# Another emission order for a fused linear-attention and SwiGLU kernel: every engine's queue and the load queue reordered, and casts, copies, masks and 1/rms dealt anew

## The chip, the cores and the metric

The kernel runs on one core of one Trainium2 chip. The core has five engines with a queue of their own each: TensorE (PE in the profile; its weight loads are PEld), VectorE (DVE), ScalarE (ACT), GpSimd (POOL) and SyncE (SP), which here only issues DMAs. The metric is the device time of one execution in microseconds, as the median of a few runs; lower is better.

## The reference

Inputs are r, k, v, w of shape (4, 8, 768, 48) (batch, heads, sequence, head size), u of (8, 48), and the weights of a feed-forward block, all in float32. The first half is a linear attention with a decaying state:

```python
for t in range(S):
    cur = einsum('bhd,bhe->bhde', u[None] * kt, vt)
    y[:, :, t] = einsum('bhd,bhde->bhe', rt, state + cur)
    state = wt[..., None] * state + einsum('bhd,bhe->bhde', kt, vt)
```

The heads are then laid side by side, which gives 3072 tokens of 384 features, and the second half is a gated block on them:

```python
rms = sqrt(mean(x * x, -1) + 1e-06); xn = x / rms * rms_g
g = xn @ w_gate; val = xn @ w_val            # 384 -> 1536
out = (g / (1 + exp(-g)) * val) @ w_out      # 1536 -> 384, float32
```

## The kernel before

**Tiling.** The sequence is cut into chunks of 128 positions, so there are six superblocks n = 0..5 of four batches j = 0..3, and a step n.j stands for one chunk of one batch with all eight heads. Four chunks (512 tokens) make one pass of the gated block, also numbered 0 to 5; in the first two passes the chunks are dealt otherwise: pass 0 takes 0.0, 0.1, 1.0 and 1.1, pass 1 takes 0.2, 1.2, 0.3 and 1.3. Pass 1 is done in halves of 256 tokens.

**Steps of a chunk.** `load_r`, `load_k`, `load_v`, `load_w` fetch 192 KB each on SP's queue (the w of superblocks 0 and 1 come together, 384 KB). `ln` takes log w on ScalarE, `cs_mm` sums it along the chunk on TensorE into two PSUM banks (from superblock 2 on into one, and VectorE's `cs_add` makes the other), `exp_r` and `exp_k` take exponentials, `r_mul` and `k_mul` scale r and k with them. The result is transposed to rkT: in superblocks 0 and 1 by TensorE (`rk_pe`) and a copy out of PSUM (`rk_tr`), later by a DMA transpose on SP's queue (`rk_tr` too). `q_mm` multiplies k by r, `q_mask_e` masks the even heads on VectorE, and the odd ones are either masked by VectorE (`q_mask_o`) or copied by ScalarE (`q_copy_o`) and then cut by GpSimd's select (`q_mask_o`). `cast_v` makes v bf16. `y_mm` adds the state's part and the chunk's own, `st_mm` and `st_new` carry the state on, `bonus_mul`, `bonus_sum` and `bonus_v` make the u term on GpSimd and VectorE, `x_add` joins them. Then come the square sum `x_sq` and `xn_mul` on ScalarE with 1/rms (`x_rstd`) between, and a transpose with the gain: `xn_pe` and `xn_out` up to superblock 3, a DMA transpose `xn_tr` on SP and `xn_gain` on GpSimd in 4 and 5.

**Steps of a pass.** For twelve groups f of 128 hidden units: `gate_mm` and `val_mm` (three matmuls of 512 columns each), `silu` on ScalarE, `h_mul` on VectorE. Then `o_mm` per chunk (twelve matmuls of 384 columns), `o_out` out of PSUM, `out_dma` on SP's queue. The last chunk's `o_mm` is in two halves, 5.3 and 5.4. The weights come by DMAs on GpSimd's queue: `load_gv.g.h` with g = 0 for groups 0 to 3, g = 1 for groups 4 to 11, h = 0 for gate and 1 for value, and `load_wo`.

**What sets the order.** ORDER is a list of 1056 steps written out; the kernel calls them in turn, so each engine, and SP's and GpSimd's DMA queues, gets its instructions in the order of its own steps in that list, and waits in that order. A suffix `:m` puts m filler matmuls on zeros ahead of the step's first PSUM use. PSUM banks come from three rings: two for gate and cs_r (`a`), two for value and cs_k (`b`), four for everything else (`q`); which bank a step gets is derived from the list. r, k and v have eight input buffers each.

**What deals the steps.** Sets of n.j name the engine: `CAST_ACT` puts `cast_v` on ScalarE (otherwise GpSimd), `K_POOL` puts `k_mul` on GpSimd (otherwise VectorE), `RK_DVE` the copy `rk_tr` on VectorE (otherwise ScalarE), `ODD_DVE` the odd mask on VectorE, `RSTD_ACT` 1/rms on ScalarE as exp(-0.5 ln) (otherwise GpSimd), `OUT_DVE` `o_out` on VectorE (otherwise ScalarE). SiLU lives in another activation table than logarithm and exponential; the helper `act` loads a table when the needed one changes.

Lines: loads 259 and 271, weight loads 351 and 354, casts 387 and 389, activations 251 with table loads 249, cs_mm 404 to 422, k_mul 459, rk_pe 482, rk_tr 487 to 491, q_mm 500 and 502, masks 507 to 518, st_mm 528, y_mm 545 and 548, 1/rms 566 and 567, xn_tr 580, groups 617 and 622 (halves), h_mul 643 and 646, o_mm 660, o_out 667 and 669, out_dma 677.

## Time and profile before

| | us |
|---|---|
| median of three runs | 204.41 (203.04 to 204.47) |
| profiled execution, first to last instruction (span) | 202.2 |
| what lies around the span, by the three runs | 0.8 to 2.3 |
| TensorE matmuls busy | 191.3 (95%) |
| VectorE busy | 157.5 (78%) |
| ScalarE busy | 135.0 (67%) |
| GpSimd busy | 124.4 (62%) |

The profiled execution's own time is its span; the runs' times also hold what lies around it, and the page does not say which of the runs it resembles most. A row of a timeline is the start, the length, the engine, the line, the operation, what it writes and reads, and in brackets the idle time ahead of it with what ended it. A row of a stretch has the length, then for each of the five engine columns PE, PEld, DVE, ACT and POOL the busy time and the number of instructions, then the granted TensorE clock, the share of the DMA engines and GB/s. In a row of groups the figures behind the first bar are busy microseconds and mean nanoseconds, behind the second the idle time ahead of the group and what ended it. A busy PE includes modelled ends of its pipelined matmuls, so its idle time is a lower bound.

### The profile page before, as it was taken

To read this page: it belongs to the slowest core of one execution; us is meant where nothing else is said; L and a number is where in the kernel's file an instruction comes from. 1 tells how busy PE (TensorE), PEld (TensorE's weight loads), DVE (VectorE), ACT (ScalarE), POOL (GpSimd) and SP (SyncE) were. 2 spreads that over 40 slices of the span, in tenths; PEclk is the share of its full clock that TensorE was granted. 3 is DMA by queue.
4 is the path that set the end of the run, shared out by engine and by line. 5 is a ranking of instruction groups with operands and counts; after the bars stand their busy time and mean duration, and the time that the engine had idled before them with its cause. 6 is when DMAs were issued, how large, how long until landed. Compare 5 with 4: busy or idle time off the path is not lost.

```text
span 202.2 us, 4604 instructions
## 1 busy us (share of the span) xinstructions
PE 191.3 (95%) x1677; PEld 121.9 (60%) x1694; DVE 157.5 (78%) x307; ACT 135.0 (67%) x278; POOL 124.4 (62%) x178
## 2 busy tenths in 40 slices
...
DMA  6999999999999998989899999995464013030132
GB/s 144 231 234 207 212 208 202 195 179 208 206 184 225 160 212 191 210 185 188 199 176 215 237 188 203 183 190 108 134 179 104 0 23 99 0 117 0 63 115 99
DMA packets 121567, 32.42 MB, mean 160 GB/s; under 512 B 116420, under 2 KB 120392, under 8 KB 121544
## 3 DMA queue, kind: packets, MB, share of 16 engines
...
q8 instruction: 13, 0.21, 0.4%
...
q10 hardware_dynamic: 8, 0.00, 0.0%
...
## 4 chain that ended last, share of the span: by engine, by line
PE 65%; ACT 3%; DMA 2%; DVE 2%; issue 1%; SPq 0%; DVEq 0%; ACTq 0%
PE ps_av L617 7%; PE ps_bu L617 7%; PE ps_au L617 7%; PE ps_bv L617 6%; PE ps_qx L660 6%; PE ps_qv L660 6%; PE ps_qu L660 5%; PE ps_qz L660 4%; PE ps_au L622 2%; PE ps_bu L622 2%; DMA rkT<-rk 2%; PE ps_av L622 2%; PE ps_bv L622 2%; ACT L249 1%; PE ps_au L419 1%; PE ps_qv L500 1%
## 5 line engine op out<-in xcount | busy, mean ns | idle before, releaser
L660 PEld LDWEIGHTS <-ht 128*128 128x128 bf16 x300 | 28.1, 98 | 17.5 <-DVE ht L646 1.0
L251 ACT ACTIVATE sg<-ps_av 128x512 bf16<-128x512 f32 x36 | 21.5, 597 | 22.8 <-PE ps_av L617 18.0
L646 DVE TENSOR_TENSOR ht<-ps_bv,sg 128x512 bf16<-128x512 f32 x29 | 19.9, 687 | 13.9 <-PE ps_bv L617 12.9
L251 ACT ACTIVATE sg<-ps_au 128x512 bf16<-128x512 f32 x36 | 21.5, 596 | 11.5 <-PE ps_au L617 7.7
L617 PEld LDWEIGHTS <-wg_sb 128*128 128x128 bf16 x180 | 19.2, 114 | 15.9 <-issue 0.6
L617 PEld LDWEIGHTS <-wv_sb 128*128 128x128 bf16 x180 | 19.2, 114 | 15.7 <-issue 0.5
L465 POOL TENSOR_TENSOR ruk<-rt,kt 128x384 f32<-128x384 f32 x24 | 24.0, 1001 | 3.7 <-DMA kt<-in_k_dram 2.8
L475 POOL TENSOR_TENSOR ydiag<-vt,diag 128x384 f32<-128x384 f32 x24 | 20.4, 859 | 9.4 <-DVE diag L470 9.1
L617 PE MATMUL ps_av<-xnt,wg_sb 128*128 128x512 bf16 x88 | 25.0, 381 | 0.3
L466 POOL TENSOR_TENSOR ruk<-ruk,u_bc 128x384 f32<-128x384 f32 x24 | 24.0, 1001 | 1.9
L617 PE MATMUL ps_bu<-xnt,wv_sb 128*128 128x512 bf16 x86 | 24.8, 380 | 0.4
L646 DVE TENSOR_TENSOR ht<-ps_bu,sg 128x512 bf16<-128x512 f32 x31 | 21.3, 686 | 4.8 <-PE ps_bu L617 3.1
L617 PE MATMUL ps_au<-xnt,wg_sb 128*128 128x512 bf16 x87 | 23.6, 380 | 0.1
L617 PE MATMUL ps_bv<-xnt,wv_sb 128*128 128x512 bf16 x82 | 23.2, 380 | 0.2
L459 POOL TENSOR_TENSOR rk<-kt,ek 128x384 bf16<-128x384 f32 x16 | 15.9, 1001 | 9.7 <-ACT ek L251 5.9
L249 ACT ACT_TABLE_LOAD x14 | 18.0, 1283 | 1.9 <-PEq L698 1.6
L660 PE MATMUL ps_qx<-wo_sb,ht 128*128 128x384 bf16 x96 | 17.1, 326 | 0.2 <-DVE ht L646 0.2
L558 ACT ACTIVATE junk<-xb 128x384 bf16<-128x384 f32 x24 | 12.5, 522 | 6.3 <-DVE xb L553 6.2
L571 ACT ACTIVATE xn<-xb,rstd 128x384 bf16<-128x384 f32 x24 | 14.2, 609 | 0.6 <-POOL rstd L567 0.5
L470 DVE TENSOR_REDUCE diag<-ruk 128x8 f32<-128x384 f32 x24 | 13.1, 544 | 1.9 <-POOL ruk L466 1.9
L660 PE MATMUL ps_qv<-wo_sb,ht 128*128 128x384 bf16 (+1 forms) x84 | 13.8, 314 | 0.0
L251 ACT ACTIVATE lw<-wt 128x384 bf16<-128x384 f32 (+1 forms) x20 | 11.6, 583 | 2.8 <-DMA wt<-in_w_dram 2.7
...
## 6 DMA issues: line engine op xcount, KB each, us to landing
...
```

What stands on the lines that cost most here:

```text
L249: nc.scalar.preload_act_table_set(table_name)
L251: return nc.scalar.activation(**kw).ins
L459: eng.tensor_tensor(out=rk[:, n % 2, j, 1, :, 0:D], in0=inp["k", n, j], in1=bank["cs_k", n, j][:, 0:DM].rearrange("p (h d) -> p h d", h=H) ...
L465: nc.gpsimd.tensor_tensor(out=ruk[n, j], in0=inp["r", n, j], in1=inp["k", n, j], op=ALU.mult)
L466: nc.gpsimd.tensor_tensor(out=ruk[n, j], in0=ruk[n, j], in1=u_bc, op=ALU.mult)
L470: nc.vector.tensor_reduce(out=diag[n, j].rearrange("p h o -> p (h o)"), in_=ruk[n, j], axis=mybir.AxisListType.X, op=ALU.add)
L475: nc.gpsimd.tensor_tensor(out=ydiag[n, j], in0=inp["v", n, j], in1=diag[n, j].to_broadcast([128, H, D]), op=ALU.mult)
L571: nc.scalar.activation(out=xn, in_=xb[n, j], func=AF.Copy, scale=rstd[n, j][:, 1:2])
L617: nc.tensor.matmul(ps, lhsT=units(ws, c, f), rhs=x[:, c, :], start=(c == 0), stop=(c == KC - 1))
L622: nc.tensor.matmul(ps[:, i * TS // 2:(i + 1) * TS // 2], lhsT=units(ws, c, f + i), rhs=x[:, c, cols], start=(i == 0 and c == 0), stop=(i = ...
L646: nc.vector.tensor_tensor(out=ht[n][:, f, :], in0=v, in1=sg, op=ALU.mult)
L660: nc.tensor.matmul(ps[:, cols], lhsT=ht[n][:, f, b * L:(b + 1) * L], rhs=wo_sb[:, f, cols], start=(f == 0), stop=(f == FC - 1))
```

## The change

ORDER is replaced by another list of the same computation, 1054 steps (the count differs because the number of odd masks that need a separate `q_copy_o` goes from 14 to 12), and six of the sets are replaced. The number of fillers stays 50, mostly at the same steps. The loads of the front begin with k.0.0 in place of r.0.0. In ScalarE's list ln.0.1 now precedes exp_r.1.0. `load_gv.0.0` (gate) precedes `load_gv.0.1` (value). In SP's list out_dma.0.2 stands ahead of several loads of superblock 2, and out_dma.5.3 ahead of out_dma.5.2. The sets end with 6 in place of 12 casts on ScalarE, 15 in place of 16 k_mul on GpSimd, 3 in place of 7 rk_tr copies on VectorE, 12 in place of 10 odd masks on VectorE, 8 in place of 7 1/rms on ScalarE, 8 in place of 14 output copies on VectorE. The commas added in Q_PAIR and OLD_DVE change nothing.

```diff
--- before.py
+++ after.py
@@ -23,106 +23,106 @@
 
 
 ORDER = """
-load_r.0.0 load_w.0.0 u_mm.0.0 ln.0.0 load_v.0.0 load_k.0.0 cs_mm.0.0:2 load_r.1.0 load_w.0.1 u_out.0.0 load_k.1.0
-load_k.0.1 load_w.0.3 load_v.0.1 exp_r.0.0 exp_k.0.0 r_mul.0.0 cast_v.0.0 load_r.0.1 bonus_mul.0.0 load_k.1.1
-bonus_sum.0.0 bonus_v.0.0 k_mul.0.0 cs_mm.1.0 load_r.1.1 load_v.1.1 load_v.1.0 load_w.0.2 rk_pe.0.0:2 rk_tr.0.0
-exp_r.1.0 w_tot.1.0 w_tot.0.0 st_mm.0.0 r_mul.1.0 st_new.0.0 q_mm.0.0:4 load_k.0.3 load_r.0.3 load_r.0.2 load_k.0.2
-load_v.0.2 ln.0.1 q_mask_o.0.0 exp_k.1.0 cs_mm.0.1 exp_r.0.1 k_mul.1.0 exp_k.0.1 rk_pe.1.0 load_v.0.3 rk_tr.1.0
-bonus_mul.1.0 q_mask_e.0.0 load_k.1.3 load_r.1.2 load_k.1.2 load_r.1.3 load_v.1.2 bonus_mul.0.1 load_w.2.1 load_w.2.0
-load_v.1.3 load_w.2.3 q_mm.1.0:2 cs_mm.1.1 exp_r.1.1 exp_k.1.1 r_mul.0.1 k_mul.0.1 w_tot.0.1 q_mask_o.1.0
-bonus_sum.1.0 load_gv.0.1 cast_v.0.1 load_r.2.0 bonus_sum.0.1 r_mul.1.1 load_w.2.2 rk_pe.0.1:2 ln.0.3 y_mm.0.0
-rk_tr.0.1 st_mm.0.1:4 x_add.0.0 q_mask_e.1.0 st_new.0.1 cs_mm.0.3:3 bonus_v.0.1 cast_v.1.0 q_mm.0.1:1 y_mm.1.0
-k_mul.1.1 bonus_v.1.0 cast_v.1.1 q_copy_o.0.1 x_sq.0.0 bonus_mul.1.1 load_r.2.1 x_add.1.0 exp_r.0.3 load_r.2.2
-x_sq.1.0 load_r.2.3 load_k.2.0 q_mask_e.0.1 w_tot.1.1 rk_pe.1.1:1 rk_tr.1.1 q_mm.1.1:7 q_mask_o.1.1 load_gv.0.0
-q_mask_o.0.1 y_mm.0.1:8 g_mm.0.0 bonus_sum.1.1 ln.0.2 x_rstd.1.0 xn_mul.1.0 x_rstd.0.0 xn_mul.0.0 exp_k.0.3
-bonus_v.1.1 load_gv.1.0 q_mask_e.1.1 x_add.0.1 x_sq.0.1 x_rstd.0.1 y_mm.1.1 x_add.1.1 k_mul.0.3 xn_pe.1.0:2 xn_pe.0.0
-cs_mm.0.2 g_out.0.0 xn_out.1.0 x_sq.1.1 xn_mul.0.1 xn_out.0.0 r_mul.0.3 st_mm.1.1:3 x_rstd.1.1 st_mm.1.0 xn_mul.1.1
-xn_pe.0.1 xn_out.0.1 w_tot.0.3 rk_pe.0.3:3 xn_pe.1.1 xn_out.1.1 exp_r.0.2 exp_k.0.2 r_mul.0.2 val_mm.0.0:4 gate_mm.0.3
-silu.0.3 val_mm.0.3 rk_tr.0.3 w_tot.0.2 st_new.1.1 load_gv.1.1 k_mul.0.2 bonus_mul.0.2 q_mm.0.3 h_mul.0.3 st_new.1.0
-gate_mm.0.2 gate_mm.0.0 rk_pe.0.2 silu.0.0 silu.0.2 val_mm.0.2 q_mask_e.0.3 h_mul.0.0 gate_mm.0.5 gate_mm.0.1 silu.0.5
-silu.0.1 val_mm.0.1 rk_tr.0.2 q_copy_o.0.3 h_mul.0.1 bonus_mul.0.3 bonus_sum.0.3 h_mul.0.2 gate_mm.0.6:1
-gate_mm.0.11:1 q_mm.0.2 cast_v.0.2 silu.0.6 silu.0.11 q_mask_o.0.2 gate_mm.0.8 val_mm.0.6 q_mask_e.0.2 cast_v.0.3
-st_mm.0.2 val_mm.0.11 q_mask_o.0.3 h_mul.0.6 val_mm.0.5 y_mm.0.3 y_mm.0.2 bonus_sum.0.2 bonus_v.0.2 load_wo.0.0
...
-silu.0.7 rk_pe.1.3 gate_mm.0.10 val_mm.0.4 h_mul.0.7 x_sq.0.2 rk_tr.1.3 load_k.2.1 load_k.2.3 load_v.2.1 load_v.2.0
-load_k.2.2 q_mm.1.2 val_mm.0.9 cast_v.1.2 xn_mul.0.3 silu.0.10 q_copy_o.1.2 h_mul.0.4 q_mask_o.1.2 gate_mm.0.9
-xn_pe.0.3 val_mm.0.10 st_new.0.3 q_mm.1.3 bonus_sum.1.2 x_rstd.0.2 q_mask_e.1.2 xn_out.0.3 y_mm.1.2 h_mul.0.10
...
-st_new.1.2 exp_k.2.2 val_mm.1.1 gate_mm.1.1 exp_r.2.2 exp_k.2.3 w_tot.2.2 val_mm.1.2 xn_pe.1.3 r_mul.2.2 gate_mm.1.2
-st_new.1.3 silu.1.1 silu.1.2 k_mul.2.0 bonus_mul.2.0 out_dma.0.0 k_mul.2.1 cast_v.2.1 k_mul.2.3 h_mul.1.1 rk_tr.2.0
...
-rk_tr.4.1 xn_mul.3.3 xn_mul.3.2 o_mm.2.1 o_mm.2.3 k_mul.4.0 xn_pe.3.1 xn_out.3.1 o_out.2.1 out_dma.2.1 cs_mm.4.2
-o_mm.2.0 r_mul.4.0 load_k.4.2 rk_tr.4.0 w_tot.4.0 bonus_sum.4.0 load_v.5.2 o_out.2.3 cs_mm.4.3 cs_add.4.2 cs_add.4.3
...
-val_mm.4.1 gate_mm.4.11 val_mm.4.3 gate_mm.4.9 h_mul.4.1 h_mul.4.3 xn_mul.5.1 x_rstd.5.2 silu.4.9 silu.4.11 xn_mul.5.2
-xn_tr.5.1 xn_tr.5.2 xn_gain.5.0 xn_gain.5.2 xn_gain.5.1 val_mm.4.9 val_mm.4.11 h_mul.4.9 h_mul.4.11 o_mm.4.3 o_mm.4.2
-o_mm.4.0 out_dma.3.0 xn_mul.5.3 xn_tr.5.3 xn_gain.5.3 gate_mm.5.1 val_mm.5.1 gate_mm.5.0 silu.5.1 silu.5.0 val_mm.5.0
...
-silu.5.11 val_mm.5.11 h_mul.5.11 out_dma.4.2 val_mm.5.6 h_mul.5.6 o_mm.5.0 o_out.4.1 out_dma.4.1 out_dma.3.1 o_mm.5.4
-o_out.5.0 o_out.5.4 out_dma.5.4 out_dma.5.0 o_mm.5.1 o_out.5.1 out_dma.5.1 o_mm.5.2 o_out.5.2 out_dma.5.2 o_mm.5.3
-o_out.5.3 out_dma.5.3
...
+load_k.0.0 load_w.0.0 u_mm.0.0 load_r.1.0 load_r.0.0 load_k.1.0 ln.0.0 cs_mm.0.0:2 load_r.0.1 load_w.0.1 u_out.0.0
+load_v.0.0 load_k.0.1 bonus_mul.0.0 load_k.1.1 load_w.0.3 exp_r.0.0 bonus_mul.1.0 load_r.1.1 load_v.0.1 load_v.1.0
+exp_k.0.0 w_tot.0.0 r_mul.0.0 k_mul.0.0 cs_mm.1.0 rk_pe.0.0:2 exp_k.1.0 ln.0.1 cs_mm.0.1 exp_r.1.0 k_mul.1.0
+load_v.1.1 exp_k.0.1 r_mul.1.0 bonus_sum.0.0 w_tot.1.0 rk_tr.0.0 cast_v.0.0 exp_r.0.1 rk_pe.1.0 load_w.0.2 cs_mm.1.1
+load_r.0.3 load_r.0.2 load_k.0.3 rk_tr.1.0 r_mul.0.1 k_mul.0.1 load_k.0.2 load_v.0.3 load_v.0.2 q_mm.0.0:4 load_r.1.2
+load_k.1.2 load_k.1.3 load_w.2.0 q_mask_e.0.0 bonus_sum.1.0 w_tot.0.1 bonus_mul.0.1 exp_k.1.1 q_copy_o.0.0 ln.0.3
+bonus_v.0.0 st_mm.0.0 rk_pe.0.1:2 q_mask_o.0.0 q_mm.1.0:2 bonus_sum.0.1 st_new.0.0 cs_mm.0.3:3 y_mm.0.0 exp_r.1.1
+load_r.1.3 load_v.1.2 q_copy_o.1.0 cast_v.0.1 k_mul.1.1 load_gv.0.0 q_mask_o.1.0 load_w.2.1 load_r.2.0 load_v.1.3
+bonus_v.1.0 r_mul.1.1 w_tot.1.1 q_mask_e.1.0 cast_v.1.0 rk_tr.0.1 x_add.0.0 rk_pe.1.1:1 y_mm.1.0 rk_tr.1.1 exp_k.0.3
+x_sq.0.0 x_add.1.0 bonus_mul.1.1 bonus_v.0.1 x_sq.1.0 q_mm.0.1:1 load_gv.0.1 x_rstd.1.0 xn_mul.1.0 x_rstd.0.0 ln.0.2
+exp_r.0.3 q_mm.1.1:7 xn_mul.0.0 q_mask_e.0.1 q_mask_o.0.1 st_mm.0.1:4 y_mm.0.1:8 q_mask_e.1.1 st_new.0.1 bonus_sum.1.1
+q_mask_o.1.1 cast_v.1.1 g_mm.0.0 x_add.0.1 r_mul.0.3 g_out.0.0 load_w.2.2 load_w.2.3 load_r.2.1 x_sq.0.1 y_mm.1.1
+xn_pe.1.0:2 bonus_v.1.1 cs_mm.0.2 xn_pe.0.0 st_mm.1.1:3 x_rstd.0.1 x_add.1.1 xn_out.1.0 k_mul.0.3 x_sq.1.1 xn_mul.0.1
+load_gv.1.0 x_rstd.1.1 xn_pe.0.1 xn_out.0.0 exp_k.0.2 xn_mul.1.1 exp_r.0.2 rk_pe.0.3:3 xn_out.0.1 xn_pe.1.1
+load_gv.1.1 xn_out.1.1 w_tot.0.2 r_mul.0.2 st_mm.1.0 val_mm.0.3:4 bonus_mul.0.2 bonus_mul.0.3 val_mm.0.0 st_new.1.0
+w_tot.0.3 gate_mm.0.3 rk_tr.0.3 silu.0.3 gate_mm.0.0 silu.0.0 gate_mm.0.1 q_mm.0.3 silu.0.1 k_mul.0.2 h_mul.0.3
+st_new.1.1 rk_pe.0.2 gate_mm.0.8 val_mm.0.1 rk_tr.0.2 h_mul.0.0 q_mm.0.2 gate_mm.0.2 silu.0.8 silu.0.2 h_mul.0.1
+q_mask_e.0.2 bonus_sum.0.2 gate_mm.0.10:1 val_mm.0.2 gate_mm.0.6:1 val_mm.0.6 q_copy_o.0.2 q_mask_o.0.2 cast_v.0.3
+bonus_sum.0.3 h_mul.0.2 q_mask_e.0.3 silu.0.6 silu.0.10 load_r.2.3 load_k.2.0 load_r.2.2 h_mul.0.6 val_mm.0.10
+bonus_v.0.3 cast_v.0.2 gate_mm.0.7 silu.0.7 h_mul.0.10 val_mm.0.8 cs_mm.1.2 st_mm.0.2 bonus_v.0.2 h_mul.0.8
+q_mask_o.0.3 st_new.0.2 exp_r.1.2 exp_k.1.2 y_mm.0.2 cs_mm.1.3 load_wo.0.0 w_tot.1.2 st_mm.0.3 y_mm.0.3 exp_k.1.3
+exp_r.1.3 ln.2.0 r_mul.1.2 k_mul.1.2 load_wo.1.0 w_tot.1.3 val_mm.0.11 x_add.0.3 r_mul.1.3 x_add.0.2 gate_mm.0.4
+rk_pe.1.2 val_mm.0.4 silu.0.4 gate_mm.0.11 bonus_mul.1.2 k_mul.1.3 rk_tr.1.2 h_mul.0.4 st_new.0.3 rk_pe.1.3
+gate_mm.0.9 silu.0.11 rk_tr.1.3 x_sq.0.3 val_mm.0.7 h_mul.0.11 q_mm.1.2 q_mask_e.1.2 h_mul.0.7 silu.0.9 q_mm.1.3
+gate_mm.0.5 val_mm.0.5 load_wo.2.0 cs_mm.2.0 val_mm.0.9 x_rstd.0.3 bonus_sum.1.2 x_sq.0.2 q_mask_e.1.3 xn_mul.0.3
+silu.0.5 h_mul.0.5 bonus_mul.1.3 q_copy_o.1.3 x_rstd.0.2 h_mul.0.9 ln.2.1 xn_mul.0.2 xn_pe.0.3 o_mm.0.3 bonus_v.1.2
+cast_v.1.2 q_mask_o.1.2 cs_add.2.0 xn_out.0.3 bonus_sum.1.3 o_out.0.3 y_mm.1.2 x_add.1.2 cs_mm.2.1 o_mm.0.0 xn_pe.0.2
+exp_k.2.0 x_sq.1.2 cast_v.1.3 q_mask_o.1.3 y_mm.1.3 x_rstd.1.2 bonus_v.1.3 cs_add.2.1 exp_r.2.0 exp_r.2.1 exp_k.2.1
+xn_mul.1.2 ln.2.2 ln.2.3 o_mm.0.2 bonus_mul.2.0 k_mul.2.0 o_out.0.0 xn_out.0.2 x_add.1.3 w_tot.2.0 r_mul.2.1 w_tot.2.1
+r_mul.2.0 st_mm.1.2 cs_mm.2.3 st_mm.1.3 xn_pe.1.2 cs_mm.2.2 o_out.0.2 load_k.2.1 out_dma.0.2 load_v.2.1 load_v.2.2
+load_k.2.2 cs_add.2.3 x_sq.1.3 cs_add.2.2 exp_k.2.3 exp_r.2.3 o_mm.0.1 xn_out.1.2 w_tot.2.3 exp_r.2.2 r_mul.2.3
...
+st_new.1.3 k_mul.2.2 val_mm.1.2 gate_mm.1.4 xn_mul.1.3 silu.1.2 h_mul.1.1 load_k.2.3 gate_mm.1.3 val_mm.1.3 xn_pe.1.3
+h_mul.1.2 bonus_mul.2.2 silu.1.3 silu.1.4 val_mm.1.5 st_mm.2.1 gate_mm.1.0 gate_mm.1.5 st_new.1.2 xn_out.1.3
...
+q_mm.3.2 load_k.4.2 bonus_v.3.3 gate_mm.2.1 cast_v.3.1 cast_v.3.3 h_mul.2.6 h_mul.2.11 q_mask_e.3.3 val_mm.2.2
...
+gate_mm.3.6 val_mm.3.3 q_mm.4.2 load_v.5.1 load_r.5.2 bonus_mul.5.0 bonus_v.4.2 h_mul.3.3 val_mm.3.8 load_v.5.3
+load_v.5.2 load_k.5.3 load_v.5.0 val_mm.3.6 q_mask_o.4.2 q_mask_o.4.3 q_mask_e.4.3 q_mask_e.4.2 ln.5.0 x_sq.4.0
+silu.3.1 x_sq.4.1 load_r.5.3 silu.3.6 bonus_mul.5.1 x_rstd.4.1 x_rstd.4.0 xn_mul.4.1 out_dma.2.0 load_w.5.3 cast_v.5.1
...
+gate_mm.4.6 x_add.5.2 h_mul.4.0 x_sq.5.2 xn_mul.5.3 xn_mul.5.1 silu.4.6 val_mm.4.9 gate_mm.4.10 val_mm.4.6 xn_gain.5.0
+x_rstd.5.2 xn_tr.5.1 xn_tr.5.3 silu.4.10 h_mul.4.9 val_mm.4.10 h_mul.4.6 h_mul.4.10 xn_mul.5.2 xn_gain.5.3 xn_gain.5.1
+o_mm.4.3 o_mm.4.2 o_mm.4.0 xn_tr.5.2 xn_gain.5.2 val_mm.5.3 gate_mm.5.5 val_mm.5.5 gate_mm.5.3 silu.5.5 silu.5.3
...
+out_dma.4.3 gate_mm.5.10 h_mul.5.0 h_mul.5.2 val_mm.5.10 silu.5.10 h_mul.5.10 o_mm.5.0 o_mm.5.1 o_out.5.0 o_out.5.1
+o_mm.5.2 o_mm.5.3 out_dma.5.0 out_dma.4.0 out_dma.5.1 o_out.5.2 o_out.5.3 out_dma.5.3 out_dma.5.2 o_mm.5.4 o_out.5.4
+out_dma.5.4
...
@@ -172,21 +172,21 @@
     def sel(s):
         return {(int(x[0]), int(x[1])) for x in s.split()}
 
-    CAST_ACT = sel("00 01 02 03 20 21 30 31 33 40 43 53")
+    CAST_ACT = sel("00 01 10 22 32 42")
     EXPR_SB = sel("")
-    K_POOL = sel("02 10 20 21 22 23 30 31 32 33 40 42 43 50 51 53")
+    K_POOL = sel("11 13 20 21 22 23 30 31 32 33 40 41 43 51 52")
     EXPK_SB = sel("02 03 10 11 12 13 20 21 22 23 30 31 32 33 40 41 42 43 50 51 52 53")
     WIN = sel("00 01 02 03 10 11 12 13")
-    Q_PAIR = ((2, 0), (2, 2), (3, 0), (3, 2), (4, 0), (4, 2), (5, 0), (5, 2))
-    OLD_DVE = (1, 2, 3, 4)
+    Q_PAIR = ((2, 0), (2, 2), (3, 0), (3, 2), (4, 0), (4, 2), (5, 0), (5, 2),)
+    OLD_DVE = (1, 2, 3, 4,)
     ONE_SUM = sel("20 21 22 23 30 31 32 33 40 41 42 43 50 51 52 53")
     XOUT_ACT = sel("")
     GAIN_DVE = sel("")
     RK_PE = sel("00 01 02 03 10 11 12 13")
-    RK_DVE = sel("00 02 03 10 11 12 13")
-    ODD_DVE = sel("00 02 10 11 13 20 23 40 43 52")
-    RSTD_ACT = sel("00 10 11 13 20 32 33")
-    OUT_DVE = sel("00 01 10 13 20 21 22 30 33 40 42 50 52 53")
+    RK_DVE = sel("00 10 12")
+    ODD_DVE = sel("01 03 11 12 20 30 33 40 42 43 50 52")
+    RSTD_ACT = sel("00 01 02 10 12 13 21 42")
+    OUT_DVE = sel("00 23 30 31 32 40 42 43")
 
     COL = {(0, 2): (1, 0), (1, 2): (1, 1), (0, 3): (1, 2), (1, 3): (1, 3), (1, 0): (0, 2), (1, 1): (0, 3)}
     HALF = (1,)
```

124 lines of the change are left out of this document (57 added, 67 removed).

## The prediction

> **What bounds the kernel now.** I read the page's first two parts, then the stretches of five microseconds, and only then single rows.
>
> ```profile
> PE 191.3 (95%) x1677; PEld 121.9 (60%) x1694; DVE 157.5 (78%) x307; ACT 135.0 (67%) x278; POOL 124.4 (62%) x178
> DMA  6999999999999998989899999995464013030132
> ...
> 0.00:5.00 5.00, 0.84 (x2) 0.49 (x2) 3.05 (x10) 1.28 (x1) 3.31 (x15) 1.00 0.62 142
> 20.00:25.00 5.00, 3.93 (x45) 2.38 (x41) 3.60 (x8) 4.12 (x13) 4.91 (x7) 1.00 1.15 214
> 120.00:125.00 5.00, 4.36 (x35) 2.38 (x34) 4.07 (x10) 3.18 (x5) 2.00 (x3) 1.00 0.96 208
> 195.00:202.00 7.00, 4.00 (x31) 2.60 (x29) 0.92 (x2) 0.48 (x1) 0.00 (x0) 0.95 0.31 114
> sum 202.00, PE 191.27 PEld 121.88 DVE 157.54 ACT 134.97 POOL 124.40; mean PE 4.78 PEld 3.05 DVE 3.94 ACT 3.37 POOL 3.11
> ```
>
> The first figure after each length is TensorE's busy time. It misses 10.7 of 202.0 us. Of these 4.2 lie in the first stretch and 3.0 in the last; the stretches from 5 to 40 us miss about 1.9 together, those from 40 to 195 about 1.6, and the two rows in the middle are the worst of each part. So matmuls bound the kernel, and whoever reorders the rest can win 3.5 us at most between 5 and 195 us, plus what the two ends give. He can lose any amount. DMA is second: its digit is 9 nearly up to 140 us, so a load queue that stands still early has to catch up later.
>
> Both orders hold the same matmuls and the same 50 filler matmuls, and counting the changes between logarithm or exponential and SiLU in ScalarE's order gives 14 table loads before and 14 after. TensorE's work is then the same, and all of the difference is in waits.
>
> **The dealing.** These rows price each move (busy us, mean ns):
>
> ```profile
> L387 ACT CAST vb<-vt 128x384 bf16<-128x384 f32 x12 | 6.1, 507 | 0.0
> L389 POOL CAST vb<-vt 128x384 bf16<-128x384 f32 x12 | 6.0, 503 | 4.4 <-DMA vt<-in_v_dram 4.4
> L459 POOL TENSOR_TENSOR rk<-kt,ek 128x384 bf16<-128x384 f32 x16 | 15.9, 1001 | 9.7 <-ACT ek L251 5.9 <-DMA kt<-in_k_dram 3.8
> L489 DVE COPY rkT<-ps_qv 128x1024 bf16<-128x1024 bf16 x3 | 2.1, 689 | 0.7 <-PE ps_qv L482 0.7
> L491 ACT COPY rkT<-ps_qv 128x1024 bf16<-128x1024 bf16 x1 | 1.0, 1013 | 0.0
> L511 ACT CAST qts<-ps_qu 128x512 bf16<-128x512 f32 x4 | 2.4, 590 | 0.0
> L515 DVE TENSOR_TENSOR qts<-ps_qu,mask_lt 128x512 bf16<-128x512 f32 x5 | 3.4, 680 | 0.0
> L518 POOL TENSOR_SCALAR_AFFINE_SELECT qts<-qts 128x512 bf16<-128x512 bf16 x14 | 8.8, 638 | 4.4 <-ACT qts L511 4.3
> L567 POOL TENSOR_TENSOR rstd<-rstd,mhalf 128x1 f32<-128x1 f32 x17 | 9.6, 563 | 1.4
> L667 DVE COPY ob<-ps_qv 128x384 f32<-128x384 f32 x4 | 2.2, 554 | 1.7 <-DMA out_dram<-ob 1.6 <-PE ps_qv L660 0.2
> L669 ACT COPY ob<-ps_qx 128x384 f32<-128x384 f32 x4 | 1.9, 476 | 1.6 <-PE ps_qx L660 1.6
> ```
>
> Net, six casts go from ScalarE to GpSimd, one k_mul from GpSimd to VectorE, four copies of transposed r and k from VectorE to ScalarE, two odd masks from a ScalarE copy with a GpSimd select to one VectorE product, six output copies from VectorE to ScalarE, one 1/rms from GpSimd to ScalarE (I put it at the 0.56 of its power step on both). ScalarE: -6 x 0.507 + 4 x 1.013 - 2 x 0.590 + 6 x 0.476 + 0.56 = +3.2 us. VectorE: one k_mul at the median of the row further down, +0.86, - 4 x 0.69 + 2 x 0.68 - 6 x 0.554 = -3.9. GpSimd: 6 x 0.503 - 1.0 - 2 x 0.638 - 0.56 = +0.2. All of it lies beside TensorE, so by itself I cost it at zero. ScalarE goes to about 138 us and VectorE to about 154, both far under 191; what the cover costs where it is missing is taken up stage by stage.
>
> The VectorE k_mul with both inputs in SBUF took 0.55 us at its shortest and 1.12 at its longest, while the one that reads PSUM took 0.55 both times:
>
> ```profile
> L459 DVE TENSOR_TENSOR rk<-kt,ek x6: 553/857/1123, 19.2 to 151.5; 128x384 bf16<-128x384 f32 x6
> L459 DVE TENSOR_TENSOR rk<-kt,ps_bu x2: 544/546/547, 9.7 to 15.0; 128x384 bf16<-128x384 f32 x2
> ```
>
> [...]
>
> **The front, up to the twelfth gate or value group (three matmuls of 512 columns).** These rows of before fix it:
>
> ```profile
> 7.08 1.00 POOL L465 TENSOR_TENSOR ruk<-rt,kt 128x384 f32<-128x384 f32 x1 [2.84 <-DMA kt<-in_k_dram]
> 9.61 0.84 ACT L251 ACTIVATE lw<-wt 128x768 bf16<-128x768 f32 x1 [0.21 <-DMA wt<-in_w_dram]
> 10.72 0.69 DVE L489 COPY rkT<-ps_qv 128x1024 bf16<-128x1024 bf16 x1 [0.52 <-PE ps_qv L482]
> 22.64 0.23 PE L500 MATMUL ps_qz<-rkT 48*128 48x128 bf16 x1 [0.85 <-DVE rkT L489]
> 25.45 0.36 PE L548 MATMUL ps_qx<-vb,qts 128*128 128x48 bf16 x8
> 30.21 0.81 PE L617 MATMUL ps_bv<-xnt,wv_sb 128*128 128x512 bf16 x2
> 27.36 0.85 POOL L351 DMA_DIRECT2D wv_sb<-in_moe_w_val_dram  x1
> 39.66 0.81 PE L617 MATMUL ps_bv<-xnt,wv_sb 128*128 128x512 bf16 x3
> DMA to landing us min/median/max: 5.5/8.5/11.5
> ```
>
> Count loads in pieces of 192 KB. Before, k.0.0 ends the fifth piece and lands at 7.08, w.0.1 ends the eighth and lands at 9.61: 0.84 us a piece. After, w.0.1 ends the ninth, so about 10.5. ScalarE now takes ln.0.1 before exp_r.1.0, so r_mul.1.0, and behind it in VectorE's order the copy rk_tr.0.0, slip: ln.0.1 to 11.3, exp_r.1.0 to 11.8, r_mul.1.0 to 12.3, bonus_sum.0.0 and w_tot.1.0 to 12.9, so rk_tr.0.0 starts near 12.9 instead of 10.72, 2.2 us later. But then k_mul.1.1 is on GpSimd (to about 17.0) and rk_tr.0.1 and 1.1 are on ScalarE, out of VectorE's queue; following ScalarE through cast_v.1.0 (v.1.0, the seventeenth piece, lands about 18), rk_tr.0.1 (1.01), exp_k.0.3 (0.4) and rk_tr.1.1 (1.01), rkT of 1.1 is ready near 20.7 and q_mm.1.1 runs at about 20.8 instead of 22.64. The chain from y_mm.1.1 through x_sq, 1/rms, xn_mul, transpose and xn_out took 4.8 us before (25.45 to 30.21); ScalarE has more in front of it now, and I give it 5.7 from 23.6, so the first val_mm starts near 29.3 instead of 30.21: -0.9.
>
> That gain stops at a DMA. The last load of gate and value weights (wv_sb, units 4 to 11) was issued at 27.36 and took 11.5 us, so it landed between 38.9 and 39.7; before first used it at 39.66, when twelve groups were done. After, its issue stands behind x_rstd.1.1 on GpSimd, by the same walk at about 27.6, so it lands at 39.1 or later, and val_mm.0.6, its first user, is already the twelfth group. Eleven groups of 0.65 with q_mm.0.3, rk_pe.0.2, q_mm.0.2 and two fillers bring TensorE there by 37.7; it waits 1.4 and has done twelve groups at 39.75, where before had them at 39.66. I take the front at +0.1, from -0.5 (the load lands by 38.5) to +1.5 (GpSimd issues it that much later).
>
> **40 to 63 us.** ScalarE's queue is dense: between gate_mm.0.7 and o_mm.0.3 it now has two table loads of 1.28, four exponentials, a logarithm, five SiLUs and the copy rk_tr.1.3. Walking it by rows, silu.0.5 ends at 51.3 and h_mul.0.9 at 52.7, where o_mm.0.3 needs them at 52.4 and 53.1. I take 0; 0.3 may be won, up to 1.5 lost if the walk is late.
>
> **The load queue at superblock 2.** In SP's order an out_dma.0.2 now stands ahead of load_v.2.1, v.2.2, k.2.2, k.2.3, v.2.3 and v.2.0, where before all but two of them stood ahead of the first output:
>
> ```profile
> 55.23 3.00 SPq L259 DMA_DIRECT2D kt<-in_k_dram  x3
> 61.98 0.78 SPq L677 DMA_DIRECT2D out_dram<-ob  x1
> 60.31 0.48 ACT L669 COPY ob<-ps_qu 128x384 f32<-128x384 f32 x1
> 74.76 0.51 POOL L389 CAST vb<-vt 128x384 bf16<-128x384 f32 x1 [1.82 <-DMA vt<-in_v_dram]
> 75.30 0.36 PE L548 MATMUL ps_qu<-vb,qts 128*128 128x48 bf16 x8
> DMA to landing us min/median/max: 3.1/3.9/7.4
> ```
>
> load_k.2.1, just ahead of it, is the 42nd piece in both orders; before issued it second in the first row, so by 57, and o_out.0.2 ran at 60.3 on ScalarE. SP now stops some 3.5 us and DMA runs dry. v.2.1 is issued near 61.5 and lands near 65.2 (the last row is that of the v loads), and GpSimd, whose next work is cast_v.2.1, waits some 2.4 us for it. Behind it stand k_mul.2.2 (to 67.6), bonus_mul.2.2 (69.7), bonus_mul.2.1 (71.7), k_mul.2.3 (72.7), bonus_mul.2.3 (74.8) and cast_v.2.0 (75.3). y_mm.2.0 wants that cast: before it ran at 75.3, and after it has one group more ahead of it. So the cover just holds; I take +0.4, between 0 and +3.0 (the whole wait).
>
> **115 to 125 us.** The only large hole after 40 us has these rows:
>
> ```profile
> 123.00 1.95 POOL L459 TENSOR_TENSOR rk<-kt,ek 128x384 bf16<-128x384 f32 x2 [3.83 <-DMA kt<-in_k_dram]
> PE ps_qu L500 <- DMA rkT<-rk: 0.6, 1, 0.6
> ```
>
> load_k.4.2 stood behind out_dma.2.1, and rk_tr.4.0 behind that load. After, load_k.4.2 is issued some 16 us of TensorE work earlier, and both k_mul of the pair come before the transposes. What is late next is rk_tr itself behind out_dma.2.1, with about 1 us to spare. I take -0.6, from -0.6 to +1.0.
>
> **The last superblock and the end.** The last x chunk is now 5.2; its 1/rms stands behind xn_gain.5.0 on GpSimd, which waits for a transpose. By rows it is in time with about half a microsecond. I take 0, up to +1.0. At the end:
>
> ```profile
> 196.60 3.17 SPq L677 DMA_DIRECT2D out_dram<-ob  x3
> 197.84 1.15 PE L660 MATMUL ps_qu<-wo_sb,ht 128*128 128x192 bf16 x12
> 199.03 0.36 DVE L667 COPY ob<-ps_qu 128x192 f32<-128x192 f32 x1 [0.38 <-PE ps_qu L660]
> ```
>
> Three outputs took SP 3.17 us with their waits. After, out_dma.5.3 is ahead of the larger and earlier out_dma.5.2, so 5.2 starts about a microsecond late and 5.4 follows it. I take +0.4, between 0 and +0.8.
>
> **Sum.** +0.1 + 0 + 0.4 - 0.6 + 0 + 0.4 = +0.3. The smaller waits left in the profile, some 1 us, are the reorderer's to win, and a new order brings its own, which no row of before shows. I bound these between -1.0 and +4.0 (six superblocks at the 0.6 of the largest hole after 40 us) and take +0.5, nearer the low end since four of the six stages walked above came out near zero. The span goes from 202.2 to 203.0; the median of the three runs, 204.41, lies 2.2 above the profiled span, and so I forecast 205.2.
>
> **Rivals.** *The load queue starves superblock 2* (chance 0.25, with other queue stops of its kind): from the point where cast_v.2.0 ends after 75.5, each microsecond is one of TensorE's; the full 3.0 in place of 0.4 gives 205.6 and a median of 207.8. For it: GpSimd already waited for a v load there before. Against: DMA is empty when the queue resumes, and loads then land in 3 to 4 us.
> *ScalarE is the bound between 30 and 63 us* (0.15): 3.2 us more work, and all four moved copies fall before 50 us. A late chain costs 1.5 there, and the value load another 1.4 over my front: 205.9, median 208.1. Against: the same stretch loses casts of v.
> *The holes close* (0.17): front -0.5, ScalarE -0.3, the hole at 120 us -0.6, the small waits -1.0, nothing lost at the queue or the end: -2.4, median 202.0. Against: every term must come out at its good end.
> *As summed, within one per cent*: 0.43. One per cent, 2 us, is about what a measurement of this kernel can tell from no change.
>
> **Numbers.** Faster by over 1%: 0.17. Within 1%: 0.43. Slower by over 1%: 0.40, both slow cases. The range, 202.0 to 209.0, leaves out the lower half of the fast case and those slow ones in which the two mechanisms meet.
>
> **What would show it.** Right: first val_mm near 29.3, val_mm.0.6 near 39.1 behind wv_sb, an SP stop of 3 to 4 us before out_dma.0.2, no 3.8 us wait of GpSimd for kt near 120, TensorE busy within 1 us of 191.3. Wrong: TensorE waits over 1 us before y_mm.2.0 or q_mm.2.2, gaps on ScalarE's SiLU before o_mm.0.3, or a front over 41 us at val_mm.0.6.

## The result

After took 205.97 us (median; 204.86 at its fastest), before 204.03 in the same comparison. The ratio is 1.0086, with a 95% interval from 1.0062 to 1.0110: slower by 0.9%, and so within the one per cent that the forecast of 205.2 us called no change. The profiled execution of after, 204.86 us with a span of 203.1, is its fastest; the other spans behind that ratio are 203.6 to 204.9. In every run recorded here the time lies 1.7 to 1.8 us above the span. In two of the experiments below (after_same_chip and out02_late) the only trace is of an execution with a mean granted clock of 0.992, and no row of it is used here.

First the page of after: busy time and the DMA digits, then the stretches of five microseconds that answer to those shown of before (length, TensorE's busy time with its instructions, then weight loads, VectorE, ScalarE, GpSimd, granted clock, DMA share, GB/s).

```profile
PE 192.6 (95%) x1694; PEld 122.0 (60%) x1694; DVE 153.8 (76%) x300; ACT 138.9 (68%) x282; POOL 124.6 (61%) x179
DMA  6999999999799998999999999981296003110232
...
20.00:25.00 5.00, 4.74 (x56) 3.11 (x51) 4.16 (x8) 4.84 (x14) 4.57 (x7) 1.00 1.09 173
80.00:85.00 5.00, 4.04 (x44) 2.76 (x41) 4.33 (x9) 3.70 (x12) 2.76 (x4) 1.00 1.05 209
120.00:125.00 5.00, 5.00 (x37) 2.56 (x36) 4.97 (x12) 4.26 (x8) 4.03 (x5) 1.00 1.07 206
150.00:155.00 5.00, 4.22 (x33) 2.10 (x32) 4.71 (x9) 3.01 (x5) 3.62 (x4) 1.00 1.27 193
```

The last two lines have to be set against before's, which were full:

```profile
80.00:85.00 5.00, 5.00 (x77) 4.19 (x76) 4.83 (x11) 4.39 (x11) 3.35 (x7) 1.00 0.85 184
150.00:155.00 5.00, 5.00 (x39) 2.62 (x38) 4.31 (x8) 4.57 (x8) 5.00 (x6) 1.00 0.38 87
```

The two poor stretches of before, 20 to 25 and 120 to 125 us, have filled up (3.93 to 4.74 and 4.36 to 5.00), and two others have opened, at 80 to 85 and 150 to 155 us. The dealing came out as worked out: ScalarE 138.9 (forecast 138), VectorE 153.8 (154), GpSimd 0.2 more (0.2).

TensorE's records are not complete in before (1677 of 1694), so its busy times cannot simply be subtracted. I used a ledger in place of that: for each TensorE step, its start in the trace less the durations of all matmuls ahead of it in its kernel's order, fillers counted as nothing; what the two kernels' ledgers differ by at equal work is what after has lost (+) or won (-) by then.

```
at (us)            33     41     63     79     87    120    129    149    158    178
after - before  -0.70  -0.49  -1.45  -1.37  -0.22  +0.01  -0.55  -0.62  +0.60  +0.96
```

After is 1.4 us ahead until 80 us. It loses 1.15 in one place at 82 us, wins 0.6 at 124 (before's hole), and loses 1.2 between 149 and 158 and 0.36 near 168. These three losses decide the difference of these two traces. That is 0.9 us of span, where the medians differ by 1.9; the other microsecond is in executions of which there is no trace. The rows of the first two, from after's timeline (start, duration, engine, line; in brackets the idle time of the engine before the row and what ended it):

```profile
81.20 0.52 ACT L251 ACTIVATE lw<-wt 128x384 bf16<-128x384 f32 x1 [1.28 <-DMA wt<-in_w_dram]
82.82 0.61 ACT L571 ACTIVATE xn<-xb,rstd 128x384 bf16<-128x384 f32 x1
83.49 0.34 PE L586 MATMUL ps_qz<-ident,xn 128*128 128x128 bf16 x3 [0.96 <-ACT xn L571]
153.40 0.23 PE L500 MATMUL ps_qz<-rkT 48*128 48x128 bf16 x1 [0.78 <-DMA rkT<-rk]
```

The first three are one chain: ln.3.0 waits 1.28 us for load_w.3.0, and behind it in ScalarE's order stand x_sq.2.1, the 1/rms and xn_mul.2.1, on whose transposes TensorE stands for 0.96 us. The last row lies inside q_mm.5.0: its first half ran at 152.2, and its second half waited for the transposed r and k of chunk 5.1. Of the 1.2 us this wait is 0.78; another 0.3 is lost at 148.80, where the first value group of pass 4 stands until ScalarE's exp_k is done. Near 168 us o_mm.4.3 ran ahead of h_mul.4.10 by 0.3 us.

### The profile page after: what moved, and what is told of

It is laid out like the page before. It is cut to its first block, busy times and chain, and to the rows that moved or that the text cites. A ratio compares the mean times of both kernels' runs of the same rounds, so it can differ in the third digit from the quotient of the medians.

```text
span 203.1 us, 4619 instructions
## 1 busy us (share of the span) xinstructions
PE 192.6 (95%) x1694; PEld 122.0 (60%) x1694; DVE 153.8 (76%) x300; ACT 138.9 (68%) x282; POOL 124.6 (61%) x179
## 4 chain that ended last, share of the span: by engine, by line
PE 59%; DMA 10%; SPq 9%; ACT 8%; POOL 7%; issue 4%; DVE 2%; ACTq 0%; DVEq 0%; POOLq 0%
PE ps_av L617 8%; PE ps_bu L617 7%; PE ps_au L617 7%; SPq L259 7%; PE ps_bv L617 6%; PE ps_qv L660 6%; PE ps_qu L660 4%; PE ps_qx L660 3%; PE ps_qz L660 3%; DMA vt<-in_v_dram 2%; DMA rkT<-rk 2%; DMA wt<-in_w_dram 2%; ACT sg L251 2%; DMA kt<-in_k_dram 2%; ACT junk L558 2%
## 5 line engine op out<-in xcount | busy, mean ns | idle before, releaser
L251 ACT ACTIVATE sg<-ps_av 128x512 bf16<-128x512 f32 x37 | 22.1, 596 | 19.6 <-PE ps_av L617 16.8
L465 POOL TENSOR_TENSOR ruk<-rt,kt 128x384 f32<-128x384 f32 x24 | 24.6, 1024 | 10.8 <-DMA kt<-in_k_dram 6.4
L251 ACT ACTIVATE sg<-ps_au 128x512 bf16<-128x512 f32 x35 | 20.8, 595 | 13.6 <-PE ps_au L617 4.5
L475 POOL TENSOR_TENSOR ydiag<-vt,diag 128x384 f32<-128x384 f32 x24 | 19.8, 829 | 2.9 <-DVE diag L470 2.9
L459 POOL TENSOR_TENSOR rk<-kt,ek 128x384 bf16<-128x384 f32 x15 | 15.1, 1017 | 3.3 <-ACT ek L251 1.8
L660 PE MATMUL ps_qu<-wo_sb,ht 128*128 128x384 bf16 x84 | 15.0, 326 | 0.1
L660 PE MATMUL ps_qv<-wo_sb,ht 128*128 128x384 bf16 x84 | 14.8, 326 | 0.0
L251 ACT ACTIVATE lw<-wt 128x384 bf16<-128x384 f32 (+1 forms) x20 | 11.5, 579 | 4.1 <-DMA wt<-in_w_dram 4.0
```

What stands on the lines that cost most here:

```text
L251: return nc.scalar.activation(**kw).ins
L459: eng.tensor_tensor(out=rk[:, n % 2, j, 1, :, 0:D], in0=inp["k", n, j], in1=bank["cs_k", n, j][:, 0:DM].rearrange("p (h d) -> p h d", h=H) ...
L465: nc.gpsimd.tensor_tensor(out=ruk[n, j], in0=inp["r", n, j], in1=inp["k", n, j], op=ALU.mult)
L475: nc.gpsimd.tensor_tensor(out=ydiag[n, j], in0=inp["v", n, j], in1=diag[n, j].to_broadcast([128, H, D]), op=ALU.mult)
L660: nc.tensor.matmul(ps[:, cols], lhsT=ht[n][:, f, b * L:(b + 1) * L], rhs=wo_sb[:, f, cols], start=(f == 0), stop=(f == FC - 1))
```

## The experiments

My theory after the result: after's losses are transfers that land late (w.3.0, rkT of 5.1), each from its place in SP's order. The rivals: stages interact, so that what is won early is given back whatever the order behind it; and the dealing costs what the order is blamed for. All ratios are against before on the same chip, with 95% intervals.

**Halves of the two orders.** Two kernels take one kernel's steps (with its dealing) up to the first value group of pass 1, and the other's remaining steps from there.

```diff
 ORDER of front_after_rest_before:  after up to
-st_new.1.3 k_mul.2.2 val_mm.1.2 ...        (rest of after)
+... st_new.1.2 val_mm.1.1 gate_mm.1.1 ...  (rest of before)
```

> The order and dealing of after up to the first value group of pass 1 (61 to 63 us), and of before from there on. The trace of after is 1.5 us ahead of before at that point. If the stages add up, that lead is kept: 204.0 - 1.5 = 202.5 us, faster than both kernels. If the load queue of before's rest gives the lead back (its loads were placed for a later arrival), it ends within 0.4 us of before, 203.6 to 204.4. If after's placing of out_dma.0.2 starves superblock 2 (the rival in the prediction), TensorE waits before y_mm.2.0 and it ends at 205 or later.

Measured: 1.0101 (1.0052 to 1.0149), slower than before.

> The other half of the pair: before up to the first value group of pass 1, after from there on. Stages that add up give after's time plus the lead it loses, 205.8 + 1.5 = 207.3 us. If after's losses behind 75 us come from its own early arrival (the load queue that cannot follow), they shrink here and it ends near 205.5.

Measured: 1.0168 (1.0123 to 1.0213). Stages that add up would have put the two ratios on both sides of 1; both halves lost instead. The second alone came out where adding puts it (207.3 over 204.0 is 1.016). After's front with before's rest loses 1.8 us in its ledger between 67 and 83 us, where neither parent does, and 1.2 more near 154. Its timeline:

```profile
72.91 0.23 PE L500 MATMUL ps_qu<-rkT 48*128 48x128 bf16 x1 [0.28 <-DMA rkT<-rk]
74.65 0.82 PE L622 MATMUL ps_au<-xnt,wg_sb 128*128 128x256 bf16 x6 [0.57 <-ACT sg L251]
155.34 0.23 PE L500 MATMUL ps_qu<-rkT 48*128 48x128 bf16 x1 [1.11 <-DMA rkT<-rk]
```

The last row is the telling one: before's own steps in superblock 5 now show the hole that I had put to after's order. So the place in the order is not what makes that transpose late.

**The dealing by itself.**

```diff
 ORDER: before's, with the sets of after
-    CAST_ACT = sel("00 01 02 03 20 21 30 31 33 40 43 53")
+    CAST_ACT = sel("00 01 10 22 32 42")
... (K_POOL, RK_DVE, ODD_DVE, RSTD_ACT and OUT_DVE likewise)
```

> Before's emission order, with casts, copies, masks and 1/rms dealt to the engines as in after (where a copy of ScalarE with a select of GpSimd becomes one product of VectorE, the product stands at the copy's place, and the other way round). The prediction costed the dealing at zero: 204.0, up to 205. The rival says that ScalarE is the bound between 30 and 63 us with the copies dealt to it: 206 to 207, with TensorE's loss in that stretch. A third case is that the dealing costs elsewhere, as k_mul.5.0 on VectorE in superblock 5: then the loss is after 140 us.

Measured: 1.0908 (1.0868 to 1.0947), 223.9 us. None of the three cases was near. From its page and timelines:

```profile
L249 ACT ACT_TABLE_LOAD x18 | 23.1, 1283 | 1.9 <-PEq L698 1.6
...
124.95 0.61 ACT L571 ACTIVATE xn<-xb,rstd 128x384 bf16<-128x384 f32 x1 [3.88 <-POOL rstd L567]
...
125.62 0.34 PE L586 MATMUL ps_qz<-ident,xn 128*128 128x128 bf16 x3 [1.70 <-ACT xn L571]
```

The moves of work that after's order takes with 1.9 us in all cost 19 us in before's. A small part of it may be the clock: all six executions had a mean granted clock of 0.985 to 0.992, before's beside them 0.997 to 1.000. In the trace the clock is halved for 3.4 us from 135.9, and that can cost 1.7 us at most. Two mechanisms show: a 1/rms dealt to ScalarE at a place among SiLUs brings table loads (18 of 1.28 us where both kernels have 14), and a 1/rms dealt to GpSimd at a place behind products of r and k makes ScalarE stand 3.88 us, with all its exponentials behind. How the 19 us divide between these and the other waits is not shown. A dealing has no price of its own; it has one in an order.

**The load w.3.0.**

```diff
-out_dma.0.3 load_w.3.3 load_k.3.0 ... load_k.3.1 load_w.3.0
+out_dma.0.3 load_w.3.0 load_w.3.3 load_k.3.0 ... load_k.3.1
```

> After, with only load_w.3.0 moved four loads earlier, ahead of load_w.3.3, load_k.3.0 and load_k.3.1. In the trace of after ScalarE waits 1.28 us for that load before ln.3.0, with x_sq.2.1, the 1/rms of 2.1 and xn_mul.2.1 behind it, and TensorE then stands 1.1 us before the transposes of xn. If that load is the cause, the wait of ScalarE goes, and after gets about 1.1 us faster: 204.7 us. If something else holds the chain (GpSimd's 1/rms, the squares), the hole stays at 82 us and the time at 205.8.

Measured: 1.0145 (1.0097 to 1.0192); after itself had 1.0086 in the first comparison and 1.0141 (below). The cause is shown and the gain is not there: the ledger's step at 82 us is +0.1 in place of +1.15 and the wait for wt is gone, but 2.2 us are lost between 95 and 104 us:

```profile
96.44 0.23 PE L500 MATMUL ps_qx<-rkT 48*128 48x128 bf16 x1 [0.66 <-DMA rkT<-rk]
97.46 0.23 PE L500 MATMUL ps_qu<-rkT 48*128 48x128 bf16 x1 [0.62 <-DMA rkT<-rk]
103.76 0.23 PE L500 MATMUL ps_qv<-rkT 48*128 48x128 bf16 x1 [0.53 <-DMA rkT<-rk]
```

load_k.3.2 was issued at 88.2 (86.5 in after), GpSimd waited 2.42 us for it before bonus_mul.3.2, and the transposes of superblock 3 came out late. In this execution the whole load queue runs 1.5 to 1.8 us behind after's first trace, and TensorE, no longer held at 82 us, meets it at 96. The lag is older than the edit: TensorE is 1.2 us later than in after by 33 us, on the very same instructions.

**The two kernels again, and the output ahead of the loads of superblock 2.**

> The kernel before, unchanged, for a trace taken on the same chip as the runs beside it. Each trace is one execution, and the first three experiments lost up to 1.3 us to the trace of after in the first 30 us with the very same instructions there. If that is the chip or the execution, this trace is late there by the same amount against the first trace of before, and has waits for loads and transposes that the first one had not. If it is their edits, this trace is the first one again, to 0.2 us.

Its one execution took 205.16 us (span 203.5). The ledger stays within 0.35 us of the first trace of before up to 105 us, so this front is repeatable here; it loses 0.6 at 107 us and has the hole at q_mm.4.0 again (0.59 us, for rkT). The three runs above were on another chip, so for them the question stays open. The other traces that begin with after's steps lie, at 41 us, between 0.2 us ahead of the first trace of before and 0.75 behind it. One thing that differs is whether TensorE meets weights that have not landed, most of all in after_loads_in_use_order:

```profile
34.93 0.84 PE L617 MATMUL ps_au<-xnt,wg_sb 128*128 128x512 bf16 x3 [0.84 <-DMA wg_sb<-in_moe_w_gate_dram]
```

> The kernel after, unchanged, as the base for the runs beside it. Expected: 1.0086 of before again, that is 1.7 us slower, and a trace that loses against before at 82 us (w.3.0), at 150 to 155 us (rkT of 5.1) and near 168 us, and is ahead until 75 us.

Measured: 1.0141 (1.0083 to 1.0198), consistent with the first comparison, the intervals overlap.

```diff
-load_k.2.1 out_dma.0.2 load_v.2.1 load_v.2.2 load_k.2.2 ... rk_tr.2.2 out_dma.0.0
+load_k.2.1 load_v.2.1 load_v.2.2 load_k.2.2 ... rk_tr.2.2 out_dma.0.2 out_dma.0.0
```

> After, with only out_dma.0.2 moved behind load_v.2.1, v.2.2, k.2.2, k.2.3, v.2.3 and the transposes 2.0 to 2.2 in SP's order, so that those loads do not wait for o_out.0.2. The prediction gave this stop +0.4 us and its rival +3.0. If the cover holds (after's trace shows no wait of TensorE before y_mm.2.0), nothing changes: within 0.5 us of after. If the stop costs, this run is 0.4 to 3.0 us faster than after. A third case: loads of superblock 3 move up as well, w.3.0 among them, and the hole at 82 us goes: 1.0 us faster.

Measured: 1.0139 (1.0043 to 1.0236): no gain against the 1.0141 of after beside it, but too wide to exclude one of a microsecond. What decides the rival is after's own trace, in the section on the forecast.

**The hole at 152 us: outputs or k_mul.**

```diff
-out_dma.2.0 load_w.5.3 ... xn_gain.4.3 xn_gain.4.0 ... xn_gain.4.2 k_mul.5.1 ... out_dma.3.0 out_dma.2.3 out_dma.3.3 ... rk_tr.5.0 rk_tr.5.1
+out_dma.2.0 out_dma.2.3 load_w.5.3 ... k_mul.5.1 xn_gain.4.3 xn_gain.4.0 ... xn_gain.4.2 ... out_dma.3.0 ... rk_tr.5.0 rk_tr.5.1 out_dma.3.3
```

> After, with three moves in superblock 5: out_dma.2.3 behind out_dma.2.0 (some 12 us earlier), k_mul.5.1 ahead of xn_gain.4.3 on GpSimd, and out_dma.3.3 behind rk_tr.5.1. In after's trace rk_tr.5.1 was issued behind three outputs and took 4.4 us to land, where before's transposes took 2.8, and TensorE waited 0.8 us for it inside q_mm.5.0. If outputs in front of the transposes are the cause, q_mm.5.0 runs without a wait and after gets 0.8 to 1.2 us faster. If it is k_mul.5.0, dealt to VectorE behind r_mul.5.1, that makes the pair late, the hole stays at over 0.5 us.

Measured: 1.0075 (1.0027 to 1.0122), against 1.0141 of after on the same chip; the intervals overlap, so a gain is not shown. The hole stays:

```profile
154.14 0.23 PE L500 MATMUL ps_qz<-rkT 48*128 48x128 bf16 x1 [0.96 <-DMA rkT<-rk]
```

By the expectation that would point to k_mul.5.0. But with k_mul.5.1 done at 146.6 and two outputs less ahead of it, rk_tr.5.1 took 4.9 us to land, even longer than the 4.4 of after, and these are counted from its issue, so a late issue is no part of them. So neither reason explains it, and what is left is the transfer itself. First how the transposes landed in the two kernels (the line of the transposes between 143 and 162 us, before, then after), then one microsecond of after and the same of before:

```profile
L487 SPq DMA_TRANSPOSE rkT<-rk x4: 1232/1248/1265, 146.6 to 153.3; - x4
DMA to landing us min/median/max: 2.7/2.8/2.8
```

```profile
L487 SPq DMA_TRANSPOSE rkT<-rk x4: 1232/1242/1548, 147.4 to 152.1; - x4
DMA to landing us min/median/max: 2.8/3.3/4.4
...
150.00:151.00 1.00, 1.00 (x7) 0.49 (x6) 1.00 (x3) 0.99 (x2) 0.92 (x2) 1.00 2.91 146
```

```profile
150.00:151.00 1.00, 1.00 (x6) 0.41 (x4) 0.65 (x2) 0.98 (x2) 1.00 (x2) 1.00 0.25 55
```

In after the packets' durations in that microsecond fill 2.91 times the 16 engines, at only 146 GB/s: few bytes for long packet times. The packet records show what stands with them: a transfer of 16 KB on the queue that the page lists as instruction. Its line is the same in both kernels:

```profile
q8 instruction: 13, 0.21, 0.4%
```

Counting TensorE's instructions (matmuls and weight loads, 3388) ahead of each of the 13, they come 252 apart on average (194 to 296 in after), the eleventh at instruction 2728 to 2761 in every trace counted. For the pair 5.0 and 5.1 the records say this (a packet of 256 bytes took 0.018 us at the median in before and in after):

```
trace                      11th transfer  held over 0.6 us         wait in q_mm.5.0
before                     150.71         none (pair done 150.24)  none
before_same_chip           151.14         none (pair done 150.95)  none
after                      150.46         23 packets of the pair   0.78
w30_earlier                154.27         23                       0.78
front_before_rest_after    153.25         22                       1.19
tr5_earlier                151.22         19                       0.96
front_after_rest_before    153.26         2 completion writes      1.11
```

The held packets begin within 0.35 us of the recorded start of the transfer, in front_before_rest_after and tr5_earlier just ahead of it. That the transfer holds them is therefore read from their meeting in each trace that has the hole, and from the next experiment, and not from the order of the records.

**Moving the instruction transfer.** Ten filler matmuls less ahead of 30 us are twenty instructions of TensorE less (`:2` ahead of a transpose stands for six of them, so the 50 fillers that the list counts are 70 matmuls). By the ledger every transfer from the third on then falls later in the work, the eleventh by 0.8 us.

```diff
-xn_pe.1.0:2 ... val_mm.0.3:4
+xn_pe.1.0 ... val_mm.0.3
```

> After without 10 of its filler matmuls (those ahead of xn_pe.1.0 and val_mm.0.3, near 25 and 29 us); the rest unchanged. The trace of after holds 13 transfers of 16 KB on the queue that the page calls instruction, one for every 252 instructions of TensorE on average. The eleventh fell at 150.46 us, into the packets of rk_tr.5.1; 23 of these took over 0.6 us where the others took 0.018, and that transpose landed 4.4 us after its issue. In before it fell 0.4 us after the last packet of its pair, which took 2.8. Ten fillers less (20 instructions of TensorE) move it some 2 us later in the work, behind rk_tr.5.1. If that collision is the cause: rk_tr.5.1 lands in 2.8, the hole inside q_mm.5.0 (0.8 us) is gone, and after gets 0.8 us faster, 1.0 to 1.8 with what the fillers themselves cost; the ninth transfer then falls on rk_tr.4.0, which has 1.5 us of cover. If the outputs ahead of the transposes or k_mul.5.0 are the cause, the hole stays.

Measured: 1.0102 (1.0068 to 1.0136). The cause is shown: the eleventh transfer now starts at 155.31, the held packets (20) belong to the next pair, which has cover, and q_mm.5.0 has no wait; the ledger's step there is +0.3 in place of +1.2, and that rest is the wait for exp_k. The time is no better than after's (1.0086 and 1.0141) all the same. The same shift has put the seventh transfer (90.95, where after's was at 88.1) on the transposes of superblock 3 (21 packets held). SP took 4.82 us to issue the first two, which after's SP did in 3.19, the other two follow late, and TensorE waits for the last; the wait for w_tot, below, is there too:

```profile
90.02 4.82 SPq L487 DMA_TRANSPOSE rkT<-rk  x2
...
103.28 0.23 PE L500 MATMUL ps_qv<-rkT 48*128 48x128 bf16 x1 [1.07 <-DMA rkT<-rk]
125.35 0.84 PE L617 MATMUL ps_au<-xnt,wg_sb 128*128 128x512 bf16 x3 [1.65 <-DVE wcol L449]
```

**The load queue in the order of use, and both.** A hole near 124 us for w_tot stands in four of the traces with after's rest, though not in after's first: r.4.3 is loaded behind six loads of superblock 5, r_mul.4.3 waits for it on VectorE (0.87 to 1.74 us), and w_tot behind that. In tr5_earlier, VectorE, then TensorE:

```profile
121.43 0.55 DVE L453 TENSOR_TENSOR rk<-rt,ps_au 128x384 bf16<-128x384 f32 x1 [0.87 <-DMA rt<-in_r_dram]
...
122.12 0.84 PE L617 MATMUL ps_au<-xnt,wg_sb 128*128 128x512 bf16 x3 [0.78 <-DVE wcol L449]
```

```diff
 (with the moves of out_dma.0.2 and load_w.3.0 above)
-load_k.4.3 load_r.5.1 ... out_dma.1.3 ... load_r.4.3
+load_k.4.3 load_r.4.3 load_r.5.1 ... out_dma.1.3
```

> After with three moves in the load queue alone: out_dma.0.2 behind rk_tr.2.2 (so that the loads of superblock 2 do not stand behind an output), load_w.3.0 ahead of load_w.3.3, k.3.0 and k.3.1, and load_r.4.3 ahead of the loads of superblock 5. If the load queue's order is what after loses by, the holes at 82 us (w.3.0) and near 123 us (r.4.3 through r_mul.4.3 and w_tot, about 1 us in all traces but the first of after) go, and DMA stays busy at 50 to 55 us: 1.0 to 2.2 us faster than after, about the time of before. If DMA is at its limit there, as moving load_w.3.0 alone suggested, the next load is late instead (k.3.2, transposes of superblock 3) and no more than 0.5 us is won.

Measured: 1.0179 (1.0120 to 1.0238). Both aimed-at holes are gone from its trace (82 us: a step of +0.07; no wait for w_tot), and others stand in their place:

```profile
71.44 0.48 ACT L669 COPY ob<-ps_qx 128x384 f32<-128x384 f32 x1 [1.08 <-DMA out_dram<-ob]
...
71.97 0.21 PE L500 MATMUL ps_qx<-rkT 48*128 48x128 bf16 x1 [0.61 <-ACT ob L669]
128.13 0.23 PE L500 MATMUL ps_qz<-rkT 48*128 48x128 bf16 x1 [1.33 <-DVE qts L507]
156.59 0.23 PE L500 MATMUL ps_qz<-rkT 48*128 48x128 bf16 x1 [0.85 <-DMA rkT<-rk]
```

The first pair explains what the early out_dma.0.2 was good for: there are three output buffers, o_out.0.1 needs the one that out_dma.0.2 frees, and q_mm.2.0 needs the PSUM bank that o_out.0.1 frees. The last row is the instruction transfer again (153.71, 23 packets held), as the fillers are untouched here.

> The three moves in the load queue and the ten fillers less together, as a version that might beat both kernels. If both causes are right and independent, 2 to 3 us faster than after and 0.5 to 1.5 us faster than before. If either gives its gain back, at before's time or above.

Measured: 1.0100 (1.0050 to 1.0151). No wait in q_mm.5.0, none at 82 us, none for w_tot; 2.5 us for that output buffer at 72.6, and rkT late at 104.5 and 129.7. Ahead of these two, 20 and 19 packets of a transpose are held once more, near 94 and 125 us, after the seventh and the ninth transfer (92.79 and 123.62). It beats neither kernel.

> Before without 10 fillers at the same two places. In before's trace the ninth instruction transfer (117.5 us) fell on the transposes of superblock 4, 15 of whose packets took over 0.6 us, and TensorE waited 0.75 us at q_mm.4.0 for rkT; the prediction put that wait to load_k.4.2 behind out_dma.2.1. Two microseconds later the transfer falls behind those packets or on the next pair. If the collision matters there, that hole shrinks and before gets 0.3 to 1.0 us faster; but the eleventh, 0.4 us behind the pair of superblock 5, moves away further and costs nothing. If the load is the cause, the hole stays and the time is before's, less at most 1.0 for the fillers.

The edit is the same two fillers taken from before. Measured: 1.0010 (0.9974 to 1.0045), no difference. The wait at q_mm.4.0 fell from 0.59 to 0.25 us, but the run does not tell the two causes apart: the ninth transfer moved from rk_tr.4.1 (117.51 in before) to rk_tr.4.0 itself (120.91), which SP took 2.69 us to issue, and some 1 us was lost elsewhere between 101 and 109. The fillers themselves cost nothing: TensorE waits where they stood (0.65 us for xnt at 30.5).

## Why the forecast held, and which steps did not

The class and the range held (205.97 against 205.2, 202.0 to 209.0), but not because the terms were right one by one; their errors cancelled, which is luck. One size in the sum's last line was off as well: I added 2.2 us from the span to the median, and in the runs it is 1.7 to 1.8. So the span of 203.0 fits after's trace, its fastest execution, and is 1.3 short of the 204.3 of the execution that gave the median. By the ledger, in the order of the sum:

- *The front*, taken at +0.1, from -0.5: -0.5 at 41 us, its lower bound, and by the reason that I gave for that bound. The first val_mm and the first user of the last weights:

```profile
29.51 0.81 PE L617 MATMUL ps_bu<-xnt,wv_sb 128*128 128x512 bf16 x3
...
38.50 0.81 PE L617 MATMUL ps_bu<-xnt,wv_sb 128*128 128x512 bf16 x3
```

  I had 29.3 and 39.1. The walk to the first val_mm was right to 0.2 us; GpSimd issued the load at 27.74 (I had 27.6); but it took 10.2 us to land where I used before's 11.5. So the wait of 1.4 us that I put there did not come: the load was in at 37.9, and TensorE, for which I had 37.7, reached it at 38.5 without a wait.
- *40 to 63 us*, taken at 0: -1.0. ScalarE was not late, the opposite of the second rival. In before o_mm.0.3 stood for the last h_mul, first row; after's ran through, second row; that is 0.3 of the 1.0 us, and the rest is in steps of under 0.3 for which I show no cause:

```profile
54.48 0.66 PE L660 MATMUL ps_qx<-wo_sb,ht 128*128 128x384 bf16 x3 [0.17 <-DVE ht L646]
```

```profile
51.38 2.11 PE L660 MATMUL ps_qv<-wo_sb,ht 128*128 128x384 bf16 x12
```
- *The load queue at superblock 2*, taken at +0.4: +0.1 between 63 and 79 us. The stop is there and shorter than my 3.5 us:

```profile
56.55 0.87 SPq L259 DMA_DIRECT2D kt<-in_k_dram  x1
59.11 0.36 SPq L677 DMA_DIRECT2D out_dram<-ob  x1
...
74.53 0.36 PE L548 MATMUL ps_qz<-vb,qts 128*128 128x48 bf16 x8
```

  1.7 us between the end of load_k.2.1 and out_dma.0.2, since o_out.0.2 came earlier than I assumed from before's 60.3; y_mm.2.0 ran without a wait. The rival that prices that stop at 3.0 is wrong at its place. Its kind, a load that SP issues too late, is what cost the 1.15 us at 82 us: I named no such place there, and the term for small waits (+0.5, up to +4.0) was all that covered it.
- *115 to 125 us*, taken at -0.6: -0.6 in after's first trace. The size was right, and so, as far as the runs tell, was the cause, load_k.4.2 and out_dma.2.1 between the two transposes; the ninth instruction transfer (at 117.51 us in before, 0.88 long), 1.2 us after whose start 15 packets of the first of them began to take over 0.6 us, may have a part in it. But the term isn't safe: in four other traces with after's rest r.4.3 costs TensorE 0.8 to 1.65 us at the same place, which may be why after's usual execution is a microsecond longer than its first trace; no run shows that. I had read the moved k load, but not the r load that the same edit sent behind six loads of the next superblock.
- *The last superblock*, taken at 0, up to +1.0: +1.2, of which 0.78 is the wait for rkT of 5.1 and 0.3 that for exp_k, and +0.36 near 168 us. This is the step that failed. I walked the x chunk 5.2 alone, to half a microsecond, and not the transposes of r and k; that their 2.8 us can be 4.4 is in no row that I quoted.
- *The end*, taken at +0.4: -0.1. out_dma.5.3 ahead of 5.2 cost nothing.

With +1.15 at 82 us, +0.2 from 87 to 120 and -0.1 from 129 to 149, these make, before rounding, the +0.9 by which the spans differ. The forecast of a small loss came out of a lead of 1.4 us, which I did not foresee, and two losses of over a microsecond each, which I did not foresee either. What did carry it was the bound in its first part: matmuls fill 95% of the span, so a reordering can win little, and it loses little unless a queue breaks, as before's order with after's dealing shows.

The VectorE k_mul with two SBUF inputs, which I counted at 0.86 us, took 0.70 us at the median in after, 0.55 at least and 1.02 at most; what sets its length no run shows.
